# W's units in one load, a new order of the first tiles, `down`'s weights spread, the last four tiles plain: an FNet and GEGLU block on one Trainium2 core

## The chip, the core and the metric

The kernel runs on one core of one Trainium2 chip. The time is device microseconds of one execution; the time before is a median of three runs. TensorE (PE in the profile) multiplies, VectorE (DVE), ScalarE (ACT) and GpSimd (POOL) do the rest, and SyncE (SP) issues every DMA from one queue. Each engine works its instructions off in the order of the program.

## The reference

```python
h  = x + Cr @ (ln(x) @ Wr.T) - Ci @ (ln(x) @ Wi.T)      # Wr, Wi: 448 x 448; Cr, Ci: 2048 x 2048
g  = ln(h) @ w_gate;  u = ln(h) @ w_up                   # 448 x 1792 each
h2 = h + (gelu_tanh(g) * u) @ w_down                     # 1792 x 448
```

x is 2048 x 448 in float32. `Wr`, `Wi` are the DFT matrices along the features, `Cr`, `Ci` those along the sequence; ln is a layer norm without weights.

## The kernel before

**Numbers.** Every product is made in fp16 from a high and a low part of each operand, as three matmuls (high by high, high by low, low by high). ScalarE makes high parts (`hi_part`, L100), VectorE low parts (`lo_part`, L104 or L106). In many places a 2 x 2 block product is made with seven products instead of eight (Strassen's way), which needs sums and differences of blocks first.

**Feature DFT (tiles F).** Sixteen tiles of 128 rows of x are loaded, normed, split (`xs`), turned (`xT`, by PE for tiles 0 to 3, by DMA after that) and multiplied with the feature DFT matrix (`wh_hi`, `wh_lo`; `feature_mm`, L404). Per tile that is 14 matmuls of 448 columns with `wh_hi` and 8 with `wh_lo`, into two banks `ab`. `feature_out` splits the result into `b`.

**Sequence DFT (units U).** Eight passes of eight units. A unit loads a block of W (`wr`, 128 x 4 x 256 float32), splits it into `ws`, and multiplies (`seq_mm`, L491): a plain unit has 24 matmuls of 448 columns, a unit of 5, 6, 7 has 42 of 224 and needs the sums `wsum` (`seq_sums`) before its split. `ws` has three buffers, `wr` four. `seq_out` ends a pass: it adds the accumulators to x in `hx`, the last two additions on GpSimd (L525). Then come the statistics of the norm, and for the first four passes norm, sums, splits and DMA transposes for the later stage.

**What sets the order there.** A list `slots` holds F tiles and units, 80 in all. `plan(n, rank, work)` puts work of the other engines ahead of slot n, by rank within a slot; the numbers in the calls of `plan` are the schedule. Between the units, the gate/up weights are made ready, 14 blocks f, each over three slots: `sums` at n, `split(True)` at n + 1, `split(False)` and the store to `w_dram` at n + 2; the raw load of the next at n + 1.

**Gate/up and down.** 56 steps t, four groups q of 512 rows with 14 blocks f each. In a step `GateUp` makes products X, Y, Z of `gw` and `hops` (L848) and combines them on VectorE (`u`, `hh`, `c`, L858), with gelu on ScalarE and two products on GpSimd. In the first 14 steps there is nothing else for PE; `down`'s weights (`wd`) are loaded, summed on GpSimd (`wd_s`), and split by `down_prep(t - 3)`, two calls per block n of seven. From step 14 on `dn_mm` (L791) multiplies by `wd` with `dn_w`, the split of the hidden tiles, seven products for two row tiles.

**The end.** The last 512 rows' four tiles of `down` are left after step 55. Two are done plainly (`last_mm`, L1011: 28 k-blocks and column halves, three matmuls each, 84 of 224 columns). The other two are a pair with seven products (`last_pair_mm`, 147 matmuls), with sums `last_v`, `last_s` and splits `last_a`.

Of the kernel before, what the change touches and what calls it, by code (L numbers as in the profile page):

```python
# [13 lines left out]
P = 128  # L14
# [18 lines left out]
def kernel(  # L33
# [157 lines left out]
    def down_load(n):  # L191
        wd32[n] = fops.tile([P, 4, HD], F32, tag="xn" if n % 2 else "tt", name=f"wd32_{n}")
        nc.sync.dma_start(wd32[n].rearrange("p (k c) d -> p k (c d)", k=2), w_down[n])
# [100 lines left out]
    first = ExitStack()  # L294
    p1 = first.enter_context(tc.tile_pool(name="p1", bufs=1, side="right"))
# [85 lines left out]
    def wh_high(k):  # L381
        hi_part(wh_hi[:, k, :], wh_raw[k // 2][:, k % 2, :], D_SC)
# [12 lines left out]
    def feature_mm(i, parts=range(2), tag="B"):  # L395
        if 0 in parts:
            feat[i] = [ps_dft.tile([P, 512], F32, tag=tag, name=f"ab{i}_{r}") for r in range(2)]
        steps = [[], [(k, wh_lo, k) for k in range(4)]]
        for k in range(4):
            steps[0] += [(k, wh_hi, k)] + ([(4 + k, wh_hi, k)] if k < 3 else [])  # L400
        for part in parts:
            for n, (kx, w, kw) in enumerate(steps[part]):
                for r in range(2):
                    PE.matmul(  # L404
                        feat[i][r][:, :D],
                        xT[i][:, kx, :],
                        w[:, kw, r * D : (r + 1) * D],
                        start=part == 0 and n == 0,
                        stop=part == 1 and n == 3,
                    )  # L410
# [44 lines left out]
    def seq_load(p, u):  # L455
        wr[p, u] = dft.tile([P, 4, 2 * P], F32, tag="wr", bufs=4, name=f"wr{p}_{u}")
        for g in range(2):
            nc.sync.dma_start(wr[p, u][:, 2 - 2 * g : 4 - 2 * g, :], w_seq[p * N_UNIT + u, :, g::2, :])

    def seq_sums(p, u):  # L460
        r = wr[p, u]
        s = wsum[p, u] = dft.tile([P, 4, 2 * P], F32, tag="wsum", bufs=2, name=f"wsum{p}_{u}")
        V.tensor_add(s[:, 0:2], r[:, 0:1].to_broadcast([P, 2, 2 * P]), r[:, 1:3])  # L463
        V.tensor_add(s[:, 2], s[:, 0], r[:, 2])
        V.tensor_add(s[:, 3], s[:, 2], r[:, 3])  # L465

    def seq_split(p, u):
        r = wr.pop((p, u))
        t = ws[p, u] = dft.tile([P, 2, 7, 2 * P], F16, tag="ws", bufs=3, name=f"ws{p}_{u}")
        parts = [(slice(0, 3), r[:, 1:4]), (slice(3, 7), wsum.pop((p, u)))] if is_s(u) else [(slice(0, 4), r)]  # L470
# [8 lines left out]
    PRODUCTS = [(1, 0, 2, 0), (2, 2, 0, 1), (6, 1, 0, 0), (0, 6, 1, 1), (3, 3, 2, 1), (5, 5, 3, 0), (4, 4, 3, 1)]  # L479

    def seq_mm(p, u, first, last):
# [4 lines left out]
        for cc in range(2):  # L486
# [11 lines left out]
            else:  # L498
                for k, a0 in ((0, 2), (1, 0)):
                    for r in range(2):  # L500
                        for m, (lb, lw) in enumerate(TERMS):
                            rhs = b[:, lb, 2 * r : 2 * r + 2].rearrange("p o d -> p (o d)")
                            mm(k, slice(0, D), w[:, lw, a0 + r, cc * P : (cc + 1) * P], rhs, end and r == 1 and m == 2)
# [8 lines left out]
    def seq_out(p):  # L512
# [11 lines left out]
        for g in range(2):  # L524
            G.tensor_add(h[:, g], h[:, g], e[:, 2 * g : 2 * g + 2].rearrange("p o d -> p (o d)"))  # L525
# [77 lines left out]
    for k, (i, i2) in enumerate(tiles_of):  # L603
        n = where["F", i]
        if k >= 2:
            plan(n - 8, 8, lambda u=i // 2: x_load(u))
            plan(n - 5, 7, lambda i=i, j=i2: x_stats(i, j))
            plan(n - 4, 5, lambda i=i, j=i2: x_rstd(i, j), lambda i=i, j=i2: x_bias(i, j))
            for c in (i, i2):
                n = where["F", c]  # L610
                plan(n - 3, 5, lambda i=c: x_norm(i), lambda i=c: x_lo(i))
                plan(n - 2, 2, lambda i=c: x_turn(i))
# [7 lines left out]
    for g, (p, u) in enumerate(units):  # L620
# [3 lines left out]
        plan(n - 2, 3, lambda p=p, u=u: seq_split(p, u))  # L624
        if g < 4:
            plan(g, 9, lambda p=p, u=u: seq_load(p, u))
# [6 lines left out]
    n0 = p1_end + 4  # L633
    order = list(reversed(range(2, NF))) + [0, 1]
    at_f = [n0 + k * (len(slots) - 3 - n0) // NF for k in range(NF)]
    plan(n0 - 3, 9, lambda: gu.update({order[0]: Weights(order[0])}))
    for k, f in enumerate(order):
# [3 lines left out]
        if k + 1 < NF:  # L641
            plan(n + 1, 9, lambda f=order[k + 1]: gu.update({f: Weights(f)}))
        plan(n + 2, 7, lambda f=f: gu[f].split(False), lambda f=f: gu[f].store())
# [16 lines left out]


    x_load(0, (slice(0, 1),))
    wh_load(0)
    x_load(0, (slice(1, 2),))
    for k in range(1, 4):
        wh_load(k)
    x_load(1)
    x_stats(0)
    wh_high(0)
    x_rstd(0)  # L670
    x_norm(0)
    x_stats(1)
    x_lo(0)
    x_turn_pe(0, 0, 4)
    wh_high(1)
    x_turn_pe(0, 4, 7)
# [3 lines left out]
    wh_high(3)  # L680
    wh_low(3, G)
    x_stats(2, 3)
    x_lo(1)
    feature_mm(0, (0,))
    x_turn_pe(1, 0, 4)
    x_turn_pe(1, 4, 7)
    x_rstd(2, 3)
    x_bias(2, 3)
    x_norm(2)
    x_lo(2)  # L690
    feature_mm(1, (0,))
# [36 lines left out]
    down_load(0)  # L728
# [553 lines left out]
```

## Time and profile before

| | |
|---|---|
| median of 3 runs | 746.25 us (745.68 to 746.96) |
| profiled execution | 745.24 us, span 743.4 us, mean granted clock 0.993 |
| PE busy | 716.3 us (96%) |
| DVE busy | 599.0 us (81%) |
| ACT busy | 329.4 us (44%) |
| POOL busy | 292.8 us (39%) |
| DMA | 142.92 MB, mean 192 GB/s; queue 60.9% busy |

A row of instructions names line, engine, operation, output and inputs, shape and count; a bracket gives the idle time before it and what ended it. "x2" is two instructions in one row. A busy PE is not PE at its full pace, since matmuls overlap; lost time shows better in how long a known number of matmuls takes.

### The profile page before, as it was taken

What the parts mean: (1) busy time and instruction counts of PE and PEld (TensorE: products, weight loads), DVE (VectorE), ACT (ScalarE), POOL (GpSimd) and SP (SyncE); (2) the same over time, 40 slices, a digit from 0 to 9 for tenths busy, and PEclk for the clock granted to TensorE, in tenths of its full rate; (3) what the DMA queues carried; (4) which work ended last, traced back from release to release, by engine and by line L of the source; (5) the groups of instructions that cost most, each with busy time, mean ns of one, the idle gap of its engine ahead of it and who ended that gap; (6) DMA issues with size and microseconds to landing.
All of it is one profiled execution on the core that took longest, in us unless ns stands there. A gap on an engine that the chain in (4) does not pass through costs nothing.

```text
span 743.4 us, 14813 instructions
## 1 busy us (share of the span) xinstructions
PE 716.3 (96%) x5779; PEld 559.1 (75%) x5779; DVE 599.0 (81%) x1165; ACT 329.4 (44%) x611; POOL 292.8 (39%) x316
## 2 busy tenths in 40 slices
PE   7999999998989999999999989999999999999987
PEld 4455557765656666677688868999999999999987
DVE  5677777898989899989447789788787877989795
ACT  5566553537363634444134444345444434444421
POOL 3033121010101020101047986577676766768460
PEclk9999999999999999999999999999999999999999
DMA  9154444788979789786167744656639475555311
GB/s 313 55 126 102 99 119 156 229 233 270 249 255 242 261 227 348 237 303 229 50 207 265 256 173 167 186 182 178 188 128 254 170 213 216 203 187 210 129 38 38
DMA packets 97927, 142.92 MB, mean 192 GB/s; under 512 B 42305, under 2 KB 81345, under 8 KB 97857
## 3 DMA queue, kind: packets, MB, share of 16 engines
q1 hardware_dynamic: 97856, 141.97, 60.9%
q8 instruction: 45, 0.74, 0.4%
q14 instruction: 26, 0.20, 0.1%
HBM read 112.46 MB, written 20.19 MB: 178 GB/s over the span
## 4 chain that ended last, share of the span: by engine, by line
PE 63%; DVE 21%; ACT 5%; DMA 4%; issue 3%; POOL 2%; SPq 1%; ACTq 0%; DVEq 0%; POOLq 0%
PE acc L491 18%; PE pY L848 12%; PE acc_d L791 11%; PE pX L848 8%; PE pZ L848 8%; PE ab L404 6%; DVE ws L106 5%; DVE gu_w L106 2%; DVE xs L104 1%; DVE wsum L463 1%; DMA x<-in_x_dram 1%; DMA gw<-w_dram 1%; DVE dn_w L104 1%; ACT ws L100 1%; DVE last_v L1032 1%
## 5 line engine op out<-in xcount | busy, mean ns | idle before, releaser
L491 PE MATMUL acc<-b,ws 128*128 128x448 f16 (+1 forms) x1968 | 282.7, 305 | 7.6 <-DVE ws L106 6.8
L491 PEld LDWEIGHTS <-ws 128*128 128x128 f16 x1968 | 188.8, 98 | 100.8 <-DVE ws L106 13.1
L848 PEld LDWEIGHTS <-gw 128*128 128x128 f16 x2067 | 202.3, 98 | 30.2 <-issue 6.5
L848 PE MATMUL pY<-hops,gw 128*128 128x256 f16 x901 | 123.2, 273 | 5.5 <-DVE u L858 5.2
L525 POOL TENSOR_TENSOR hx<-hx,e 128x448 f32<-128x448 f32 x16 | 25.2, 1594 | 253.3 <-DVE e L522 158.6
L791 PE MATMUL acc_d<-wd,dn_w 128*128 128x224 f16 x882 | 105.4, 259 | 0.0
L106 DVE SCALAR_TENSOR_TENSOR ws<-wr,ws 128x1024 f16<-128x1024 f32 (+1 forms) x64 | 76.7, 1199 | 15.0 <-ACT ws L100 14.8
L791 PEld LDWEIGHTS <-dn_w 128*128 128x128 f16 x882 | 85.2, 98 | 3.0
L100 ACT ACTIVATE ws<-wr 128x1024 f16<-128x1024 f32 (+1 forms) x64 | 61.6, 969 | 50.1 <-PE acc L491 25.2
L848 PE MATMUL pX<-hops,gw 128*128 128x256 f16 x583 | 81.3, 273 | 1.7 <-DMA gw<-w_dram 1.7
L848 PE MATMUL pZ<-hops,gw 128*128 128x256 f16 x583 | 79.7, 274 | 0.0
L858 DVE SCALAR_TENSOR_TENSOR u<-pY,u 128x256 f32<-128x256 f32 x112 | 47.0, 420 | 36.6 <-PE pY L848 18.2
L886 ACT ACTIVATE u<-pX 128x256 f32<-128x256 f32 x56 | 21.4, 382 | 90.4 <-PE pX L848 84.9
L404 PEld LDWEIGHTS <-xT 128*128 128x128 f16 x352 | 34.4, 99 | 34.3 <-issue 2.3
L915 POOL TENSOR_TENSOR hh<-hh,g 128x256 f32<-128x256 f32 x42 | 35.9, 855 | 57.8 <-DVE hh L858 57.8
L104 DVE TENSOR_TENSOR dn_w<-dn_s,dn_w 128x640 f16<-128x640 f32 x42 | 52.7, 1254 | 1.6 <-ACT dn_w L100 1.4
L899 ACT ACTIVATE g<-pX 128x256 f32<-128x256 f32 x56 | 21.3, 380 | 70.0 <-PE pX L848 66.5
L404 PE MATMUL ab<-wh_hi,xT 128*128 128x448 f16 x224 | 47.0, 360 | 1.1 <-DVE b L106 0.7
L100 ACT ACTIVATE ws<-wsum 128x1024 f16<-128x1024 f32 x24 | 25.3, 1054 | 50.9 <-DVE wsum L465 50.9
L941 POOL TENSOR_TENSOR dn_s<-hh 128x256 f32<-128x256 f32 x42 | 43.5, 1036 | 0.0
L924 POOL TENSOR_TENSOR hh<-hh,c 128x256 f32<-128x256 f32 x42 | 36.8, 877 | 16.3 <-ACT c L922 16.3
L942 POOL TENSOR_TENSOR dn_s<-hh 128x256 f32<-128x256 f32 x42 | 43.1, 1026 | 0.0
(134 smaller groups left out, 956.8 us busy)
## 6 DMA issues: line engine op xcount, KB each, us to landing
gw<-w_dram SPq DMA_DIRECT2D x53, 896.0 KB, 5.0
wr<-in_w_seq_dram SPq DMA_DIRECT2D x128, 256.0 KB, 4.9
w_dram<-gu_w SPq DMA_DIRECT2D x14, 896.0 KB, 4.8
gu_raw<-in_w_gu_dram SPq DMA_DIRECT2D x28, 384.0 KB, 4.7
wd<-in_w_down_dram SPq DMA_DIRECT2D x14, 448.0 KB, 4.9
hx<-in_x_dram SPq DMA_DIRECT2D x8, 448.0 KB, 5.8
h_dram<-hx SPq DMA_DIRECT2D x8, 448.0 KB, 5.2
hr<-h_dram SPq DMA_DIRECT2D x8, 448.0 KB, 5.4
```

What stands on the lines that cost most here:

```text
L100: A.activation(dst, src, AF.Copy, scale=scale)
L104: V.tensor_sub(dst, src, hi)
L106: V.scalar_tensor_tensor(dst, src, scale, hi, op0=ALU.mult, op1=ALU.subtract)
L404: PE.matmul(feat[i][r][:, :D], xT[i][:, kx, :], w[:, kw, r * D : (r + 1) * D], start=part == 0 and n == 0, stop=part == 1 and n == 3,)
L491: PE.matmul(banks[k][:, cols], lhs, rhs, start=k not in begun, stop=stop, skip_group_check=True)
L791: PE.matmul(acc[k // 2][:, k % 2 * HD : (k % 2 + 1) * HD], a_of(la, a), b_of(lb, b), start=first and m == 0 and k % 2 == 0, stop=last and ...
L848: PE.matmul(ps, w[:, wl, wa + ws, :], ops[:, m + ms, :], start=first and n == 0, stop=last and n == len(terms) - 1, skip_group_check=True,)
L858: V.scalar_tensor_tensor(dst, ps, SC, other, op0=ALU.mult, op1=ALU.add)
L915: G.tensor_mul(c21, c21, self.g1)
L924: G.tensor_mul(c22, c22, self.c12)
L941: G.tensor_add(s[:, 0:2], t[:, 0:2], t[:, 2:4])
L942: G.tensor_sub(s[:, 2:4], t[:, 1:4:2], t[:, 0:4:2])
```

## The change

- Each unit of W comes in one DMA of 512 KB in the order in which it lies in memory, instead of two; the quarters are named anew in `seq_sums`, `seq_split`, `PRODUCTS` and `seq_mm`, and a unit with sums is split in three pieces instead of two.
- `feature_mm` of one tile is cut into eleven steps in place of two parts; at the start PE's order mixes the steps of tiles 0, 1, 2 with the turns of tiles 1, 2, 3. GpSimd makes the fourth block of `wh_hi`, the first two tiles of x are loaded ahead of all of `wh`, and x loads, statistics, norms and turns of later tiles are planned two slots earlier.
- One gate/up block's weights are made ready among the feature tiles (slot 14); the other thirteen follow from slot 24 on, the last at slot 71 instead of 73. The raw load moves from n + 1 to n + 2 and the store from n + 2 to n + 3.
- `seq_out`'s last two additions run on VectorE.
- `down`'s first load and sums stand in the sequence passes; `down_prep` runs two steps earlier.
- The last four tiles of `down` are all made by `last_mm`; the pair's code is gone.

```diff
-    def feature_mm(i, parts=range(2), tag="B"):
+    def feature_mm(i, part=range(11), tag="B"):
...
+        steps = [(k, wh_hi, n) for k, n in ((0, 0), (1, 1), (4, 0), (5, 1), (2, 2), (6, 2), (3, 3))]
+        steps += [(k, wh_lo, k) for k in range(4)]
...
     def seq_load(p, u):
         wr[p, u] = dft.tile([P, 4, 2 * P], F32, tag="wr", bufs=4, name=f"wr{p}_{u}")
-        for g in range(2):
-            nc.sync.dma_start(wr[p, u][:, 2 - 2 * g : 4 - 2 * g, :], w_seq[p * N_UNIT + u, :, g::2, :])
+        nc.sync.dma_start(wr[p, u], w_seq[p * N_UNIT + u])
...
-        parts = [(slice(0, 3), r[:, 1:4]), (slice(3, 7), wsum.pop((p, u)))] if is_s(u) else [(slice(0, 4), r)]
+        parts = [(slice(0, 1), r[:, 0:1]), (slice(1, 3), r[:, 2:4]), (slice(3, 7), wsum.pop((p, u)))] if is_s(u) else [(slice(0, 4), r)]
...
         for g in range(2):
-            G.tensor_add(h[:, g], h[:, g], e[:, 2 * g : 2 * g + 2].rearrange("p o d -> p (o d)"))
+            V.tensor_add(h[:, g], h[:, g], e[:, 2 * g : 2 * g + 2].rearrange("p o d -> p (o d)"))
...
-    n0 = p1_end + 4
+    pairs = [where["F", 2 * u] for u in ORDER if is_s(u)]
+    early_f = [s + 4 for s in pairs[1:2]]
+    n0 = p1_end + 3
...
         plan(n + 1, 7, lambda f=f: gu[f].split(True))
         if k + 1 < NF:
-            plan(n + 1, 9, lambda f=order[k + 1]: gu.update({f: Weights(f)}))
-        plan(n + 2, 7, lambda f=f: gu[f].split(False), lambda f=f: gu[f].store())
+            plan(n + 2, 9, lambda f=order[k + 1]: gu.update({f: Weights(f)}))
+        plan(n + 2, 7, lambda f=f: gu[f].split(False))
+        plan(n + 3, 10, lambda f=f: gu[f].store())
...
+    plan(len(slots) - 14, 9, lambda: down_load(0))
+    plan(len(slots) - 8, 9, lambda: down_sums(0))
...
-    wh_high(3)
+    x_lo(1)
     wh_low(3, G)
-    x_stats(2, 3)
-    x_lo(1)
-    feature_mm(0, (0,))
+    feature_mm(0, range(6))
+    x_stats(2)
     x_turn_pe(1, 0, 4)
     x_turn_pe(1, 4, 7)
...
-            if t == 2:
-                down_sums(0)
-            if t > 2:
-                down_prep(t - 3)
+            if t > 0:
+                down_prep(t - 1)
...
-        if t - 3 <= 2 * NC:
-            down_prep(t - 3)
+        if t == 2 * NC:
+            down_prep(t - 1)
...
+    for n, (j, g) in enumerate(((0, 0), (0, 1), (1, 0))):
+        last_mm(j, g, banks[n : n + 1])
         do(N_GU + 1 + n, 3)
...
-        last_pair_mm(n)
...
+        last_out(j, g, banks[n], 0, 2)
+    last_mm(1, 1, banks[3:])
```

The end of pass 2 on VectorE before: `acc2` are the pass's banks, `hx2` its rows, `e2` helper sums, `ws3` and `wsum3` the next pass's W.

```order
L520 SCALAR_TENSOR_TENSOR hx2_1870<-acc2_1_1753,hx2_1870 128x448
L521 SCALAR_TENSOR_TENSOR e2_2139<-acc2_3_1755,e2_2139 128x224
L522 SCALAR_TENSOR_TENSOR e2_2139<-acc2_2_1754,e2_2139 128x224
L523 SCALAR_TENSOR_TENSOR e2_2139<-acc2_2_1754,e2_2139 128x224
L106 SCALAR_TENSOR_TENSOR ws3_1_2149<-wr3_1_1976,ws3_1_2149 128x1024
L463 TENSOR_TENSOR wsum3_6_2152<-wr3_6_2011 128x512
L464 TENSOR_TENSOR wsum3_6_2152<-wsum3_6_2152,wr3_6_2011 128x256
```

The same place on VectorE now (lines are three further down):

```order
L523 SCALAR_TENSOR_TENSOR hx2_1885<-acc2_1_1774,hx2_1885 128x448
L524 SCALAR_TENSOR_TENSOR e2_2154<-acc2_3_1776,e2_2154 128x224
L525 SCALAR_TENSOR_TENSOR e2_2154<-acc2_2_1775,e2_2154 128x224
L526 SCALAR_TENSOR_TENSOR e2_2154<-acc2_2_1775,e2_2154 128x224
L528 TENSOR_TENSOR hx2_1885<-hx2_1885,e2_2154 128x448 x2
L106 SCALAR_TENSOR_TENSOR ws3_1_2164<-wr3_1_1998,ws3_1_2164 128x1024
L466 TENSOR_TENSOR wsum3_6_2167<-wr3_6_2031 128x512
```

The two additions (L528) now stand on VectorE ahead of the split of the next unit; before, they were GpSimd's and ran beside that split.

VectorE at steps 14 and 15 of gate/up before: `wd` is written by a low part of `down`'s weights, `dn_w` by one of the hidden tiles, `u3` and `u2` are what PE waits for.

```order
L106 SCALAR_TENSOR_TENSOR wd_4085<-wd_s_5_4927,wd_4085 128x1120
L104 TENSOR_TENSOR dn_w1_5017<-hh0_4106,dn_w1_5017 128x256
L104 TENSOR_TENSOR dn_w1_5017<-dn_s1_4944,dn_w1_5017 128x640
L858 SCALAR_TENSOR_TENSOR u3_14_5047<-pY_14_4965,u1_14_4978 128x256
L858 SCALAR_TENSOR_TENSOR hh1_4999<-pZ_14_5003,u3_14_5047 128x256
L943 TENSOR_TENSOR dn_s2_5050<-hh0_4106 128x128
L217 SCALAR_TENSOR_TENSOR nb_h2_0_5065<-mv_h2_0_3019,r_h2_0_3028 128x2
L858 SCALAR_TENSOR_TENSOR hh1_4999<-pY_14_4965,u1_14_4978 128x256
L858 SCALAR_TENSOR_TENSOR c12_14_5081<-pZ_14_5003,u2_14_4980 128x256
L858 SCALAR_TENSOR_TENSOR u2_15_5102<-pY_15_5087,u1_15_5100 128x256
L106 SCALAR_TENSOR_TENSOR wd_4085<-wd32_6_4925,wd_4085 128x448
L104 TENSOR_TENSOR dn_w2_5120<-hh0_4106,dn_w2_5120 128x256
```

The same place on VectorE now:

```order
L106 SCALAR_TENSOR_TENSOR wd_4080<-wd_s_6_4926,wd_4080 128x1120
L104 TENSOR_TENSOR dn_w1_5012<-hh0_4101,dn_w1_5012 128x256
L104 TENSOR_TENSOR dn_w1_5012<-dn_s1_4943,dn_w1_5012 128x640
L882 SCALAR_TENSOR_TENSOR u3_14_5042<-pY_14_4964,u1_14_4977 128x256
L882 SCALAR_TENSOR_TENSOR hh1_4998<-pZ_14_5002,u3_14_5042 128x256
L967 TENSOR_TENSOR dn_s2_5045<-hh0_4101 128x128
L217 SCALAR_TENSOR_TENSOR nb_h2_0_5060<-mv_h2_0_3023,r_h2_0_3032 128x2
L882 SCALAR_TENSOR_TENSOR hh1_4998<-pY_14_4964,u1_14_4977 128x256
L882 SCALAR_TENSOR_TENSOR c12_14_5076<-pZ_14_5002,u2_14_4979 128x256
L882 SCALAR_TENSOR_TENSOR u2_15_5097<-pY_15_5082,u1_15_5095 128x256
L104 TENSOR_TENSOR dn_w2_5112<-hh0_4101,dn_w2_5112 128x256
```

At step 14 a `wd` split still stands ahead of `dn_w1` (block 6's in place of block 5's); at step 15 the one ahead of `dn_w2` is gone, and so is step 16's.

161 lines of the change are left out of this document (68 added, 93 removed).

## The prediction

> **What bounds the kernel now.** I read the busy times stage by stage first, then who TensorE (PE) waited for, then the order of time at those places. The stages: the first three feature tiles, the rest of the feature DFT, the later sequence passes, the first gate/up block, the other blocks, the end. Columns of the first six rows: the stretch, its length, busy time of PE, its weight loads, VectorE (DVE), ScalarE (ACT) and GpSimd (POOL), the granted clock, DMA.
>
> ```profile
> 0.00:27.20 27.20, 21.46 (x144) 12.93 (x145) 13.25 (x40) 15.33 (x27) 5.90 (x10) 0.94 0.67 230
> 27.20:104.50 77.30, 76.45 (x445) 43.08 (x443) 58.65 (x124) 45.75 (x73) 20.16 (x18) 1.00 0.42 101
> 156.80:289.00 132.20, 124.80 (x872) 82.57 (x871) 120.59 (x228) 61.31 (x93) 13.34 (x8) 1.00 0.88 255
> 371.60:465.00 93.40, 86.68 (x781) 76.53 (x779) 68.00 (x131) 39.68 (x85) 65.89 (x69) 0.98 0.61 213
> 465.00:704.80 239.80, 239.31 (x2289) 222.12 (x2288) 198.82 (x400) 102.23 (x242) 163.39 (x188) 1.00 0.59 189
> 704.80:743.40 38.60, 32.72 (x318) 30.74 (x315) 29.17 (x57) 7.49 (x12) 14.53 (x17) 0.96 0.10 37
> ...
> 104.50:138.60 34.10, 34.10 (x244) 23.47 (x243) 1.00 0.52 158
> ...
> PE acc L491 <- DVE ws L106: 6.8, 16, 1.1
> PE pY L848 <- DVE u L858: 5.2, 5, 2.3
> PE acc_d L791 <- DVE last_a L104: 3.0, 3, 2.1
> PE pX L848 <- DMA gw<-w_dram: 1.7, 2, 1.3
> ```
>
> PE bounds the kernel, and what it loses is lost at five places. From 465 to 704.8 us it loses nothing, and the change does not touch that. In the sequence passes an undisturbed stretch ran 244 matmuls in 34.10 us; the 872 of 156.8 to 289 us need 872 x 34.10 / 244 = 121.9 us at that pace and took 132.2. So 10.3 us are lost there, more than the wait rows name, and there VectorE is busy 120.6 of 132.2 us, the rest being its own waits: VectorE is the bound of that stretch. In the first gate/up block PE waits for VectorE's `u`, at the end for `last_a`.
>
> **The end (last four tiles plain): -3.4 us.**
>
> ```profile
> 704.74 8.05 PEld L1011 LDWEIGHTS <-h_last 128*128 128x128 f16 x84
> 718.08 2.49 PE L791 MATMUL acc_d<-wd,last_a 128*128 128x224 f16 x13 [2.14 <-DVE last_a L104]
> ...
> 710.00:720.00 10.00, 7.86 (x73) 7.07 (x72) 9.90 (x16) 2.21 (x3) 8.27 (x10) 0.91 0.06 20
> ...
> 732.43 4.03 PE last_X L1011 x42
> 736.45 4.04 PE last_Y L1011 x42
> ```
>
> One plain tile is 84 matmuls of 224 columns and takes 8.05 us, paced by its weight loads. Before, the end held two such tiles and, for the other two, seven products of 21 matmuls, 147 in all; now it holds four plain tiles, 336 matmuls for 315. The 21 more cost 2.0 us. But the pair now needs no sums and splits (VectorE 9.90 of 10 us in the row, with waits of PE up to 2.14 us and a clock of 0.91 behind them). Four tiles from 704.8 us take 4 x 8.05 = 32.2 us, to 737.0; before, the last tile ended at 736.45 + 4.04 = 740.5. What follows it (a half tile's sum, a store) is the same. Nothing is late next: the last hidden tile's low part is needed at the end of the first plain tile, as before.
>
> **Passes' sums to VectorE, W in one load: -3.0 us.** Each pass ends with two additions that move from GpSimd to VectorE (instructions L525).
>
> ```profile
> 158.00 3.20 POOL L525 TENSOR_TENSOR hx<-hx,e 128x448 f32<-128x448 f32 x2 [31.32 <-DVE e L522]
> ...
> 158.08 2.13 DVE L106 SCALAR_TENSOR_TENSOR ws<-wr,ws 128x1024 f16<-128x1024 f32 x1
> 160.13 1.62 DVE L463 TENSOR_TENSOR wsum<-wr 128x512 f32<-128x512 f32 x1
> 162.59 0.55 DVE L543 TENSOR_TENSOR gu_s<-gu_raw 128x384 f32<-128x384 f32 x1
> 186.87 1.22 DVE L106 SCALAR_TENSOR_TENSOR ws<-wr,ws 128x1024 f16<-128x1024 f32 x1
> 188.00 0.69 DVE L463 TENSOR_TENSOR wsum<-wr 128x512 f32<-128x512 f32 x1
> 189.52 1.28 DVE L106 SCALAR_TENSOR_TENSOR gu_w<-gu_s,gu_w 128x512 f16<-128x512 f32 x2
> ```
>
> While GpSimd adds, the same VectorE instructions take 2.13 and 1.62 us that take 1.22 and 0.69 elsewhere: 0.91 + 0.93 = 1.84 us. The additions on VectorE have 448 columns, between 384 (0.55) and 512 (0.69): 0.62 each, less the overlap of neighbours, 1.15 for two. VectorE gains 0.7 us at a pass end; the eight POOL instructions of the stretch are four such ends: 2.8 us. Against it, a unit with sums is now split in three pieces instead of two: two pieces of 512 take 1.28, one of 1024 takes 1.22, so about 0.07 more for each of some 11 units: 0.8 us. ScalarE's extra piece lies in its 61 busy of 132 us. Of the gate/up weights' preparation one unit moves into the feature stage and the others shift by a slot, which takes about a quarter of a unit (L543 to its last split, some 4 us by these rows) out of the stretch: 1.0 us. Together 2.8 - 0.8 + 1.0 = 3.0. Ends: all 10.3 us if VectorE's waits for ScalarE go too; a loss of 4 x 1.15 + 0.8 = 5.4 if the stretching has another cause and stays. I stay with the row that shows it.
>
> The Trainium skill ("SBUF — State Buffer", on the shared port pair) says that GpSimd and a VectorE instruction with two SBUF inputs take the pair exclusively and the loser blocks for the whole instruction. By that, each end would cost 3.2 us and the gain were 4 x (3.2 - 1.15) = 8.2 instead of 2.8, the sum 5.4 lower; the row shows 1.84 of 3.2, so the trace agrees on the contention, not on the full block.
>
> One DMA per unit of W instead of two halves SyncE's issues; no PE wait there names a load, and of VectorE's four kinds of wait in the stretch the second row below is the only one for a DMA, so I cost the merged load at nothing: the four buffers that run ahead cover it, and without them a landing is some 5 us. The weights' raw load moves one slot later, the store behind it another; the next sums stand two slots on, two units of the 8 in a pass of 34 us, some 8 us, and the load lands in 4.7 (last column of the first row).
>
> ```profile
> gu_raw<-in_w_gu_dram SPq DMA_DIRECT2D x28, 384.0 KB, 4.7
> ...
> DVE gu_s L543 <- DMA gu_raw<-in_w_gu_dram: 0.5, 1, 0.5
> ```
>
> **First tiles' order: -2.3 us.**
>
> ```profile
> 9.97 1.79 ACT L100 ACTIVATE wh_hi<-wh_raw 128x896 f16<-128x896 f32 x2
> 11.12 0.63 DVE L314 BATCH_NORM_STATS2 st_x<-x 128x6 f32<-128x448 f32 x1 [1.97 <-DMA x<-in_x_dram]
> 11.85 2.44 POOL L390 TENSOR_SCALAR wh_raw<-wh_raw 64x896 f32<-64x896 f32 x1 [9.60 <-ACT wh_hi L100]
> 24.48 0.39 PE L369 MATMUL xT_ps<-ident,xs 128*128 128x128 f16 x4
> 27.23 2.81 PE L404 MATMUL ab<-wh_hi,xT 128*128 128x448 f16 x14
> ...
> 58.65 8.29 PE ab L404 x43
> ```
>
> Tile 3 began at 27.23 us. Now PE puts tile 1's and 2's transposes between matmuls, and the fourth block of the hidden DFT's high part is made by GpSimd: it stands for 2.44 us (the nearest row has the same width on half the partitions). Its data landed by 10.8, since ScalarE worked on it without a wait; more likely about 10. So PE passes that matmul pair at 12.5 to 13.3. By then 12 of the 66 matmuls of tiles 0 to 2 are done; 54 remain at 8.29 / 43 = 0.193 us, 10.4 us, and two turns of seven transposes, about 0.6 each by the row and its sibling. 12.8 + 10.4 + 1.2 = 24.4, and 0.5 for small waits: 24.9, so -2.3. Ends: 0 if VectorE's chain of statistics for tiles 2 and 3 (they wait for x at 11.12) sets the pace, -3.5. The rest of the feature stage loses 0.85 us of PE now; x, norms and turns come two slots earlier, one gate/up unit (4 us of VectorE, 58.65 busy of 77.30) is added, and I leave it as it is, within 1 us either way.
>
> **Gate/up's first block: -2.3 us.**
>
> ```profile
> 373.10 0.38 DVE L523 SCALAR_TENSOR_TENSOR e<-acc,e 128x224 f32<-128x224 f32 x1
> 374.14 0.82 PE L848 MATMUL pY<-hops,gu_w 128*128 128x256 f16 x6
> 376.00 1.04 SPq L193 DMA_DIRECT2D wd<-in_w_down_dram  x2
> 384.78 0.83 PE L848 MATMUL pX<-hops,gw 128*128 128x256 f16 x6 [1.30 <-DMA gw<-w_dram]
> 441.89 1.23 PE L848 MATMUL pY<-hops,gw 128*128 128x256 f16 x5 [2.29 <-DVE u L858]
> 446.92 1.25 DVE L106 SCALAR_TENSOR_TENSOR wd<-wd,wd 128x448 f16<-128x448 f32 x1
> 450.69 0.71 PE L848 MATMUL pY<-hops,gw 128*128 128x256 f16 x5 [0.78 <-DVE u L858]
> 453.99 1.61 DVE L106 SCALAR_TENSOR_TENSOR wd<-wd_s,wd 128x1120 f16<-128x1120 f32 x1
> 458.12 0.71 PE L848 MATMUL pY<-hops,gw 128*128 128x256 f16 x5 [1.00 <-DVE u L858]
> ```
>
> `down`'s splits run two steps earlier. At steps 15 and 16 the `wd` splits of 1.25 and 1.61 us vanish from VectorE's queue ahead of `u`, and with them the waits of 0.78 and 1.00: -1.8. The wait of 2.29 us at step 14 stays: a `wd` split and `dn_w` stand ahead of `u` as before. One of the two `down` loads at 376.0 moves ahead, so the weights that PE waited 1.30 us for get the queue sooner: -1.3. But the last pass's two additions now stand on VectorE between L523 and the first `u`: 1.15 us, and PE's second pY of 374.14 needs it at once: +0.8. GpSimd's first `wd_s` sums go into the sequence passes, where it is idle.
>
> **Sum.** -3.4 - 3.0 - 2.3 - 2.3 = -11.0 us on the profiled execution of 745.24 us (span 743.4, 1.84 around it), which is 734.2; the median of the runs lies 1.01 higher: 735.2 us.
>
> **Rivals.** (a) The passes gain nothing, because pieces and additions give back what GpSimd's absence brings: 738.2. For it: the terms are small against 132 us; against it: the stretched rows. (b) VectorE gets ahead and its waits for ScalarE go with it, most of the 10.3 us: 728 to 731. For it: a queue that is full; against it: the norm's chain through ScalarE is unchanged. The clock belongs here: the skill's "TensorE: Matmul & The Clock Gate" (part 1, the clock gate) has windows of 3.4 us that run freely and half rate after one idle window; the trace fell to half after waits of only 2.14 and 2.29 us. As the phase is free, the fall behind step 14's wait may go, 1.7 us less, 733.5; I count it to the range. (c) The start gains nothing or the feature stage pays it back: 737.5 to 739. (d) Slower: in the stretch that VectorE bounds, every sum of gate/up weights waits for its raw load, now issued a slot later behind SyncE's queue. Seven units stand there; from 1.6 us of wait each it eats all 11.0, and at 2 us the time is 749. One such wait of 0.5 us exists now; against it stands the distance of some 8 us to a landing of 4.7.
>
> **How the numbers follow.** The forecast with its parts near their values: 0.62; (a) 0.14; (b) 0.10; (c) 0.08; (d) 0.06, of which 0.04 end slower and 0.02 within the bound. Less than 0.2% of the time (1.5 us) is about what a measurement of this kernel cannot tell from no change. Faster by more 0.94, within 0.02, slower 0.04. The range from 731 to 740 leaves out (d), and the further half of (b).
>
> **What would show it.** End: 84 weight loads in 8.05 us four times over, clock 1.00, no wait for `last_a`. Passes: no L525 on POOL, `ws` at 1.22 behind `seq_out`, fewer than 10.3 us lost. Start: tile 3 near 25 us. First block: no waits at steps 15 and 16, 2.3 us at 14, and a new one below 1 us at the first pY. Wrong would make it: new waits of VectorE for `gu_raw`, or of PE in the feature stage.

## The result and the profile after

The changed kernel takes 738.66 us (736.13 to 740.09, four runs) where the kernel before, in four runs, takes 746.40: a ratio of 0.9891 with a 95% interval of 0.9875 to 0.9908. The forecast was 735.2 us in a range of 731 to 740. The profiled execution is the shortest of the four, 736.13 us with a span of 734.3. For half of the four the mean granted clock is 0.998 and for half 0.993, which fits the half rate described at the end of this document: it comes in some runs and not in others.

The stages of the profile after, cut at the same events as in the table below (columns as in the prediction's first fence: stretch, length, busy time of PE, its weight loads, VectorE, ScalarE, GpSimd, granted clock, DMA):

```profile
0.00:28.56 28.56, 20.90 (x144) 13.34 (x145) 18.34 (x57) 13.98 (x27) 8.79 (x11) 0.94 0.58 210
28.56:111.64 83.08, 81.13 (x467) 45.33 (x466) 59.15 (x120) 47.83 (x80) 20.48 (x18) 1.00 0.50 126
111.64:370.07 258.43, 254.14 (x1789) 172.02 (x1788) 227.50 (x447) 117.17 (x190) 4.28 (x3) 1.00 0.73 233
370.07:434.10 64.03, 62.02 (x565) 55.02 (x564) 46.83 (x93) 27.66 (x60) 44.13 (x46) 1.00 0.69 238
434.10:698.92 264.82, 262.02 (x2504) 243.05 (x2502) 219.47 (x441) 114.12 (x267) 181.21 (x208) 1.00 0.58 187
698.92:734.30 35.38, 32.36 (x338) 32.11 (x336) 6.28 (x12) 1.20 (x3) 6.85 (x10) 1.00 0.11 40
```

| stage | before | after | difference | forecast |
|---|---|---|---|---|
| until tile 3's first matmul | 27.23 | 28.56 | +1.33 | -2.3 |
| from there to slot 22 (feature stage) | 81.65 | 83.08 | +1.43 | 0, within 1 |
| slots 22 to 79 (passes) | 262.75 | 258.43 | -4.32 | -3.0 |
| gate/up steps 0 to 13 | 64.88 | 64.03 | -0.85 | -0.5 |
| from the first `dn_mm` (step 14) to the end's first matmul | 268.33 | 264.82 | -3.51 | -1.8 |
| the end | 38.56 | 35.38 | -3.18 | -3.4 |
| span | 743.4 | 734.3 | -9.1 | -11.0 |

Whom PE waited for, after (waited for, total, times, longest); the first row is new in this size, and `last_a` and the DMA of `gw` are gone:

```profile
PE xT_ps L370 <- ACT xT L371: 5.8, 4, 2.3
PE pY L872 <- DVE u L882: 4.5, 4, 2.3
PE acc L494 <- DVE ws L106: 4.4, 10, 0.7
PE ab L408 <- DVE b L106: 1.7, 4, 0.9
```

The start, timeline of after. Of VectorE's two splits of `wh` in the second row the first takes 2.02 us, beside a GpSimd instruction (first row), and the other its usual 1.08. VectorE reaches the statistics of tiles 10 and 11 late, and ScalarE's square root `sd_x` for them waits 2.24 us. Behind it in ScalarE's queue stand `b` of tile 0 and the copy `xT` of tile 3's turn, for which PE waits 2.34 us:

```profile
16.43 1.99 POOL L396 TENSOR_TENSOR wh_lo<-wh_raw,wh_hi 64x896 f16<-64x896 f32 x1
17.35 3.02 DVE L106 SCALAR_TENSOR_TENSOR wh_lo<-wh_raw,wh_hi 128x896 f16<-128x896 f32 x2
...
24.43 0.29 ACT L121 ACTIVATE sd_x<-mv_x,eps_t 128x2 f32<-128x2 f32 x1 [2.24 <-DVE mv_x L316]
24.63 0.96 ACT L100 ACTIVATE b<-ab 128x448 f16<-128x448 f32 x2
25.48 0.60 ACT L371 ACTIVATE xT<-xT_ps 128x512 f16<-128x512 f16 x1
26.13 0.33 PE L370 MATMUL xT_ps<-ident,xs 128*128 128x128 f16 x3 [2.34 <-ACT xT L371]
```

The feature stage, at the border of slots 10 and 11, repeats it: ScalarE stood 3.76 us before a square root, its part of `feature_out` came behind, and PE waited 0.89 us for the bank.

```profile
63.19 0.29 ACT L121 ACTIVATE sd_x<-mv_x,eps_t 128x2 f32<-128x2 f32 x1 [3.76 <-DVE mv_x L316]
63.40 0.96 ACT L100 ACTIVATE b<-ab 128x448 f16<-128x448 f32 x2
64.63 0.35 PE L408 MATMUL ab<-wh_hi,xT 128*128 128x448 f16 x1 [0.89 <-DVE b L106]
```

The end of pass 2 on VectorE, after: the two additions, then the split and the sum at their usual 1.22 and 0.69 us, not 2.13 and 1.62.

```profile
160.61 1.15 DVE L528 TENSOR_TENSOR hx<-hx,e 128x448 f32<-128x448 f32 x2
161.68 1.22 DVE L106 SCALAR_TENSOR_TENSOR ws<-wr,ws 128x1024 f16<-128x1024 f32 x1
162.81 0.69 DVE L466 TENSOR_TENSOR wsum<-wr 128x512 f32<-128x512 f32 x1
```

The last wait of gate/up's first block, at step 14, and the weight loads of all four last tiles (a group: count, busy time, mean ns): 32.2 us, four times 8.05.

```profile
439.48 0.70 PE L872 MATMUL pY<-hops,gw 128*128 128x256 f16 x5 [2.29 <-DVE u L882]
```

```profile
L1035 PEld LDWEIGHTS <-h_last 128*128 128x128 f16 x336 | 32.2, 98 | 0.0
```

### The profile page after: what moved, and what is told of

Its sections match the earlier page's. It is cut to its first block, busy times and chain, and to the rows that moved or that the text cites. A ratio compares the mean times of both kernels' runs of the same rounds, so it can differ in the third digit from the quotient of the medians.

```text
span 734.3 us, 14677 instructions
## 1 busy us (share of the span) xinstructions
PE 712.6 (97%) x5800; PEld 560.9 (76%) x5800; DVE 577.6 (79%) x1166; ACT 322.0 (44%) x624; POOL 265.7 (36%) x294
## 4 chain that ended last, share of the span: by engine, by line
PE 65%; DVE 19%; ACT 7%; DMA 4%; issue 4%; POOL 2%; SPq 1%; ACTq 0%; DVEq 0%; POOLq 0%
PE acc L494 19%; PE pY L872 13%; PE acc_d L815 11%; PE pX L872 8%; PE pZ L872 8%; DVE ws L106 4%; DVE xs L104 2%; ACT ws L100 2%; DMA w_dram<-gu_w 2%; DVE gu_w L106 2%; ACT b L100 2%; DMA x<-in_x_dram 1%; PE last_Z L1035 1%; PE last_X L1035 1%; PE last_tr L1035 1%
## 5 line engine op out<-in xcount | busy, mean ns | idle before, releaser
L198 POOL TENSOR_TENSOR wd_s<-wd 128x448 f32<-128x448 f32 x7 | 8.0, 1144 | 217.0 <-DMA wd<-in_w_down_dram 217.0
L106 DVE SCALAR_TENSOR_TENSOR ws<-wr,ws 128x1024 f16<-128x1024 f32 (+2 forms) x88 | 74.6, 871 | 14.8 <-ACT ws L100 14.2
L100 ACT ACTIVATE ws<-wr 128x1024 f16<-128x1024 f32 (+2 forms) x88 | 63.7, 756 | 49.3 <-issue 30.3
```

The source lines that it names most:

```text
L100: A.activation(dst, src, AF.Copy, scale=scale)
L106: V.scalar_tensor_tensor(dst, src, scale, hi, op0=ALU.mult, op1=ALU.subtract)
```

## The experiments

The first nine kernels alter the changed kernel in one thing or two; the last three build on one another. A ratio is against runs of the kernel before on the same chip. "Tile 3" and "slot 22" are their first matmuls in the one profiled execution of each kernel; "steps 14 on" runs to the end's first matmul. Since there is one profile for each kernel, the columns show how far they repeat: the passes lie between 258.37 and 258.58 us in the six kernels that change nothing there, but tile 3 begins between 28.13 and 29.47 in the six that have the changed start, and between 26.41 and 28.75 in the three that share start_no_gpsimd's. A single difference of 1 or 2 us at tile 3 shows little.

| kernel | median, us (lowest to highest) | ratio to before, 95% | tile 3 | slot 22 | passes | steps 14 on |
|---|---|---|---|---|---|---|
| before | 746.40 (745.68 to 746.96) | | 27.23 | 108.88 | 262.75 | 268.33 |
| after | 738.66 (736.13 to 740.09) | 0.9875 to 0.9908 | 28.56 | 111.64 | 258.43 | 264.82 |
| start_undone | 735.55 (734.39 to 736.18) | 0.9834 to 0.9871 | 28.89 | 110.54 | 258.58 | 265.06 |
| stats_late | 742.09 (739.93 to 743.36) | 0.9926 to 0.9961 | 26.16 | 113.79 | 258.53 | 266.26 |
| x_in_slots | 737.82 (733.97 to 740.45) | 0.9848 to 0.9901 | 27.73 | 110.95 | 258.42 | 264.82 |
| x_in_slots_wh3_act | 738.96 (737.95 to 739.70) | 0.9881 to 0.9907 | 29.31 | 112.53 | 258.42 | 266.30 |
| sums_gpsimd | 742.39 (740.51 to 744.24) | 0.9929 to 0.9964 | 28.13 | 111.33 | 262.67 | 266.57 |
| gu_undone | 737.98 (737.30 to 738.43) | 0.9874 to 0.9905 | 28.60 | 111.26 | 259.92 | 264.80 |
| w_two | 746.28 (742.91 to 748.67) | 0.9970 to 0.9999 | 29.47 | 114.28 | 263.39 | 264.90 |
| w_two_gu_undone | 738.20 (737.63 to 738.47) | 0.9869 to 0.9907 | 28.43 | 111.08 | 259.94 | 264.82 |
| down_undone | 740.88 (739.35 to 741.57) | 0.9908 to 0.9934 | 29.24 | 110.96 | 258.81 | 268.31 |
| start_no_gpsimd | 735.67 (734.79 to 736.98) | 0.9834 to 0.9875 | 27.72 | 109.36 | 258.37 | 266.30 |
| units_moved | 728.93 (727.88 to 731.32) | 0.9744 to 0.9791 | 26.41 | 108.05 | 251.99 | 266.30 |
| down_earlier | 727.95 (726.10 to 730.06) | 0.9730 to 0.9767 | 28.75 | 110.40 | 251.99 | 263.44 |

### The start and the feature stage

**start_undone.** The hand-written order, the plan of x and W's first loads as before:

```diff
-    feature_mm(0, range(6))
-    x_stats(2)
+    x_stats(2, 3)
+    x_lo(1)
+    feature_mm(0, range(7))
...
-                plan(n - 7, 7, lambda i=i, j=i2: x_stats(i, j))
+            plan(n - 5, 7, lambda i=i, j=i2: x_stats(i, j))
```

> The changed kernel with the order of the first tiles, the plan of x and the first loads of W as before; all else of the change stays. Theory A (the new order of the start costs the 1.3 us at tile 3 and the 1.4 us of the feature stage, since the norms of later tiles stand ahead of feature_out on ScalarE and VectorE): tile 3 begins near 27.2 us instead of 28.5, the waits of slots 10, 11 fall to those of before, the span is 2.7 us shorter (near 731.6 where the clock dips no more often). Rival B (the gate/up unit that moved among the feature tiles, or W in one load, costs the 1.4 us): tile 3 at 27.2, but the feature stage from there to slot 22 still 83 us long, the span 1.3 shorter.

The interval lies wholly below that of the changed kernel: by the medians the new start costs 3.1 us. In the profile the feature stage is back at 81.65 us, with the early gate/up unit and the single load of W still there. So theory A holds for the feature stage and rival B falls. Tile 3, however, begins at 28.89, not at 27.2, in the old order, so the profile does not show where the rest of the 3.1 us lies. At this start the last of VectorE's small steps for tile 2's and 3's `r_x` took 1.73 us beside an instruction of GpSimd; the group's row (least, median and most of nine, in ns) has 0.16 us for its median:

```profile
13.96 1.91 POOL L396 TENSOR_TENSOR wh_lo<-wh_raw,wh_hi 64x896 f16<-64x896 f32 x1
...
14.16 1.73 DVE L132 SCALAR_TENSOR_TENSOR r_x<-r_x 128x2 f32<-128x2 f32 x1
```

```profile
L132 DVE SCALAR_TENSOR_TENSOR r_x<-r_x x9: 158/160/1728, 5.2 to 85.3; 128x2 f32<-128x2 f32 x7, 128x1 f32<-128x1 f32 x2
```

**stats_late.** The copies of tile 3's turn ahead of tile 0's `feature_out` and of the statistics of tiles 10 and 11:

```diff
-    x_stats(a, b)
-    x_rstd(a, b)
-    x_bias(a, b)
...
-    feature_out(0)
     feature_mm(1, range(7, 9))
     x_turn_pe(3, 0, 4)
     x_turn_pe(3, 4, 7)
+    feature_out(0)
+    x_stats(a, b)
+    x_rstd(a, b)
+    x_bias(a, b)
```

> The changed kernel; at the start the statistics of tiles 10 and 11 and tile 0's feature_out stand behind tile 3's turn, no longer ahead of it. Theory A1 (ScalarE's copies of tile 3's turn wait in its queue behind a square root that VectorE feeds late): PE's wait of 2.34 us there falls to about 0.7, tile 3 begins at 26.9 us instead of 28.5, the span is 1.6 us shorter. Rival A2 (VectorE's work of the start, drawn out by GpSimd's instructions beside it, sets the pace wherever the statistics stand): tile 3 moves by less than 0.5 us, and the wait turns up at feature_out's bank.

Tile 3 did begin 2.4 us earlier, at 26.16, and 2.0 earlier than in any kernel that has the changed start: A1 is right on what delayed it. But the run is 3.4 us slower. The statistics now come late for the norm of tile 10 on ScalarE, the norms stand ahead of the first split of W, and PE waits 3.04 us for that split at slot 4. From 33.8 us on the clock is at half for 3.4 us, and the feature stage is 4.6 us longer in all:

```profile
29.03 0.76 ACT L336 ACTIVATE x<-x,nb_x,r_x 128x448 f32<-128x448 f32 x1 [1.02 <-DVE nb_x L328]
...
32.43 1.04 ACT L100 ACTIVATE ws<-wr 128x1024 f16<-128x1024 f32 x1
...
33.52 0.70 PE L494 MATMUL acc<-b,ws 128*128 128x448 f16 x2 [3.04 <-ACT ws L100]
```

**x_in_slots.** The mixed start kept; x from the third pair on planned as before, `wh_load(0)` second:

```diff
-    a, b = tiles_of[2]
-    x_stats(a, b)
-    x_rstd(a, b)
-    x_bias(a, b)
...
-                plan(n - 4, 2, lambda i=c: x_turn(i))
+                plan(n - 2, 2, lambda i=c: x_turn(i))
```

> The changed kernel with its mixed order of tiles 0 to 3 at the start, but with the x tiles from the third pair on in the plan of before (load, statistics, norm and turn 8, 5, 3 and 2 slots ahead), wh's first block loaded ahead of the second tile of x as before, and tile 3's turn ahead of feature_out(0). Theory A (two things cost: the norms planned two slots earlier, and at the start what stands ahead of the copies on ScalarE): tile 3 begins at 26.3 us or up to 0.7 earlier, the feature stage from there is 81.7 us long as before, slot 22 begins near 108 instead of 111.6, the run is 3.5 us faster than the changed kernel. Rival: the waits in the feature stage come with W in one load or the early gate/up unit; then slots 10, 11 still lose 1.4 and 0.3 us and slot 22 begins near 109.5.

The losses of slots 10 and 11 shrink as theory A says (1.39 and 0.34 to 0.34 and 0), but tile 3 begins at 27.73 and tile 10's turn is late at slot 5 (last row), so that the feature stage still takes 83.22 us, against 83.08. By the times it is not told apart from the changed kernel. Two `xs` splits of VectorE that take 0.69 us elsewhere took 2.37, again beside L396:

```profile
15.08 1.87 POOL L396 TENSOR_TENSOR wh_lo<-wh_raw,wh_hi 64x896 f16<-64x896 f32 x1
15.14 2.37 DVE L104 TENSOR_TENSOR xs<-x,xs 128x64 f16<-128x64 f32 x2
...
38.23 2.06 PE L408 MATMUL ab<-wh_hi,xT 128*128 128x448 f16 x10 [1.63 <-DMA xT<-xs]
```

**x_in_slots_wh3_act.** In addition `wh_high(3)` on ScalarE:

```diff
-    wh_high(3, G)
...
+    wh_high(3)
```

> As x_in_slots, and ScalarE makes the fourth block of wh_hi, as before, not GpSimd. If GpSimd's longer work at the start (2.78 us for that block, then the low part) draws out VectorE's splits of wh (1.51 us each against 1.03) and its small steps, VectorE reaches the statistics of tile 3 about 1 us earlier and tile 3 begins up to 1 us earlier than in x_in_slots. If PE does not wait for VectorE there any more: no difference at tile 3 (within 0.3 us).

Tile 3 begins 1.6 us later, with a stretch of half clock of 3.4 us ahead of it that the other profile does not have. Half of that stretch, 1.7 us, is the whole difference. GpSimd's L396 only hits another instruction of VectorE, a split of `wh` that takes 1.08 us elsewhere:

```profile
13.95 1.90 POOL L396 TENSOR_TENSOR wh_lo<-wh_raw,wh_hi 64x896 f16<-64x896 f32 x1
14.03 2.76 DVE L106 SCALAR_TENSOR_TENSOR wh_lo<-wh_raw,wh_hi 128x896 f16<-128x896 f32 x1
```

### The passes

**sums_gpsimd.**

```diff
-            V.tensor_add(h[:, g], h[:, g], e[:, 2 * g : 2 * g + 2].rearrange("p o d -> p (o d)"))
+            G.tensor_add(h[:, g], h[:, g], e[:, 2 * g : 2 * g + 2].rearrange("p o d -> p (o d)"))
```

> The changed kernel with seq_out's last two additions on GpSimd again. By the prediction's row (GpSimd draws out VectorE's neighbours by 1.84 us, the two additions on VectorE cost 1.15) the passes from slot 22 on get 2.8 us longer over four pass ends that PE feels; by a full block of VectorE 8.2 us longer; if the additions are worth nothing, 0, and then the 4.3 us that the passes gained come from the other parts.

4.24 us longer, between the two prices. The row is back as it was: 1.84 us more on VectorE's two instructions at each pass end.

```profile
161.05 3.20 POOL L528 TENSOR_TENSOR hx<-hx,e 128x448 f32<-128x448 f32 x2 [30.70 <-DVE e L525]
161.13 2.13 DVE L106 SCALAR_TENSOR_TENSOR ws<-wr,ws 128x1024 f16<-128x1024 f32 x1
163.19 1.61 DVE L466 TENSOR_TENSOR wsum<-wr 128x512 f32<-128x512 f32 x1
```

**gu_undone.**

```diff
-    early_f = [s + 4 for s in pairs[1:2]]
-    n0 = p1_end + 3
+    n0 = p1_end + 4
...
-            plan(n + 2, 9, lambda f=order[k + 1]: gu.update({f: Weights(f)}))
-        plan(n + 2, 7, lambda f=f: gu[f].split(False))
-        plan(n + 3, 10, lambda f=f: gu[f].store())
+            plan(n + 1, 9, lambda f=order[k + 1]: gu.update({f: Weights(f)}))
+        plan(n + 2, 7, lambda f=f: gu[f].split(False), lambda f=f: gu[f].store())
```

> The changed kernel with the gate/up weights' preparation placed as before (no unit among the feature tiles, fourteen from slot 25 on, load and store a slot earlier). By the prediction the passes lose 1.0 us of their gain. Rival: where a unit stands against a pass end decides, not the sum of VectorE's work; then the losses move to other slots and the passes change by 2 us or more in either direction. The wait of 0.42 us at slot 21 should go only if the early unit causes it.

The passes are 1.49 us longer, the feature stage 0.42 shorter, for the wait at slot 21 is gone. That is near the forecast's 1.0; the losses did move among the slots, but not by 2 us in sum. In the medians the two cannot be told apart.

**w_two.**

```diff
-        nc.sync.dma_start(wr[p, u], w_seq[p * N_UNIT + u])
+        for g in range(2):
+            nc.sync.dma_start(wr[p, u][:, 2 - 2 * g : 4 - 2 * g, :], w_seq[p * N_UNIT + u, :, g::2, :])
```

> The changed kernel with W in two loads per unit and in the old order of its quarters, two pieces to a split instead of three. By the prediction the third piece costs 0.8 us in the passes and the loads nothing: the passes get 0.8 us shorter, the feature stage stays. Rival: 64 more DMA issues on SyncE's queue make other transfers late (gu_raw, x), and VectorE or PE waits for them: 1 us or more longer.

The surprise of the study: 746.28 us, nearly all of the change's gain gone. In the profile the passes are 5.0 us longer, the feature stage 1.7, the first steps of gate/up 1.4 and the start 0.9. In the passes VectorE waits for gate/up's raw weights (columns as in PE's waits), here at 236.55 us, and PE behind it for `ws`:

```profile
DVE gu_s L547 <- DMA gu_raw<-in_w_gu_dram: 7.2, 5, 2.1
```

```profile
236.55 0.56 DVE L547 TENSOR_TENSOR gu_s<-gu_raw 128x384 f32<-128x384 f32 x1 [2.07 <-DMA gu_raw<-in_w_gu_dram]
...
243.02 1.31 PE L495 MATMUL acc<-b,ws 128*128 128x448 f16 x6 [1.41 <-DVE ws L106]
```

In the changed kernel the same wait is 0.4 us in all. This is rival (d) of the prediction, in its place and with its mechanism; W's single load keeps it off.

The 1.7 us of the feature stage are another wait, all of them in slots 19 to 21. There ScalarE writes a feature tile (`b`, as `b32` in the code) into a buffer that it shares (tag `w`) with the early gate/up block's weights, and it may start only when these are stored to `w_dram`. With two loads of W that store comes later. PE then waits 0.85 us for the tile and 0.69 for the next split; in the changed kernel only 0.24 at that split are left of it.

```profile
103.88 0.98 ACT L100 ACTIVATE b<-ab 128x448 f32<-128x448 f32 x2 [9.37 <-DMA w_dram<-gu_w]
104.47 3.05 PE L408 MATMUL ab<-wh_hi,xT 128*128 128x448 f16 x14 [0.85 <-ACT b L100]
```

**w_two_gu_undone.** Both of the last two edits.

> The changed kernel with both W in two loads (as in w_two, whose passes were 5.0 us longer) and the gate/up preparation placed as before (as in gu_undone, 1.5 us longer). Theory I (the one load is worth nothing by itself, it only covers the gate/up raw load that now stands a slot later behind SyncE's loads of W): with the raw load early again VectorE's waits for gu_raw fall from 7.2 us to under 1, and the passes take 259 to 260 us. Rival II (two loads per unit cost by themselves, as SyncE or the DMA engines are slower with them): 5.0 + 1.5 us over the changed kernel's 258.4, 264 to 265.

Theory I: 259.94 us, as gu_undone's 259.92. With the gate/up plan of before, two loads and two pieces take as long as one load and three pieces; load and piece were not changed apart, so a small cost of the one could hide a small gain of the other. One wait for `gu_raw` is left, longer than expected (gu_undone has one of 1.0):

```profile
DVE gu_s L547 <- DMA gu_raw<-in_w_gu_dram: 1.6, 1, 1.6
```

Whether SyncE's issues or the transfers themselves delay the raw load behind two loads of W was not separated: in w_two a unit's issue takes 1.21 us where one load takes 0.33, and the raw load's median time to landing is 6.0 us, against 5.3 in the changed kernel.

### Down's weights

**down_undone.**

```diff
-            if t > 0:
-                down_prep(t - 1)
+            if t == 2:
+                down_sums(0)
+            if t > 2:
+                down_prep(t - 3)
```

> The changed kernel with down's first load behind the passes, its first sums at step 2 and down_prep(t - 3) again. By the prediction the waits of 0.78 and 1.00 us at steps 15 and 16 come back, and the wait for gate/up's weights behind down's second load (1.30 us): together 3.1 us longer, up to 1.7 more or less where the clock's dip behind step 14 differs. Rival: steps 15 and 16 wait for something else, or the two loads collide no more: under 1 us.

From step 14 on it takes 3.5 us more, though the clock does not dip there in either profile; the two waits are 1.56 and 1.00 us, and one of 0.64 for `hh` comes with them. PE never waits for `gw`, although `down`'s load stands behind the passes again: that part of the expectation is wrong.

```profile
442.04 0.81 PE L871 MATMUL pY<-hops,gw 128*128 128x256 f16 x6 [0.64 <-DVE hh L881]
448.00 0.71 PE L871 MATMUL pY<-hops,gw 128*128 128x256 f16 x5 [1.56 <-DVE u L881]
455.43 0.71 PE L871 MATMUL pY<-hops,gw 128*128 128x256 f16 x5 [1.00 <-DVE u L881]
```

### Towards a faster kernel

**start_no_gpsimd.** start_undone without GpSimd at the start:

```diff
-    wh_low(3, G)
...
-    for k in range(3):
+    for k in range(4):
         wh_low(k)
```

> As start_undone, and VectorE makes the low part of wh's fourth block, so that GpSimd does nothing between 3 and 30 us. Theory (in start_undone GpSimd's TENSOR_TENSOR of 1.91 us held a VectorE step of 0.16 us for 1.73 us, and this chain set tile 3's start): no step of r_x longer than 0.2 us, tile 3 at 27.3 us (1.4 earlier) unless the clock dips there. Rival: the fourth low part on VectorE (about 1.03 us) makes it late for xs of tile 3, and tile 3 begins no earlier than 28.3.

No `r_x` step is drawn out, and GpSimd has nothing to do at the start after its first memory fill. Tile 3 begins at 27.72 us with 3.4 us of half clock around 11 us, at 26.41 in the next kernel, which has the same start and no dip there, and at 28.75 in the last, with a dip from 15.3 us on. The times show no difference from start_undone (735.67 against 735.55): the stall of that profile is not shown to cost on average.

**units_moved.** In addition the gate/up blocks' slots by hand:

```diff
-    at_f = early_f + [n0 + k * (len(slots) - 5 - n0) // late_f for k in range(late_f)]
+    at_f = [14, 20, 24, 30, 37, 45, 53, 56, 59, 62, 65, 68, 71, 74]
...
-            plan(n + 2, 9, lambda f=order[k + 1]: gu.update({f: Weights(f)}))
+            plan(n + (1 if at_f[k + 1] - n < 4 else 2), 9, lambda f=order[k + 1]: gu.update({f: Weights(f)}))
```

> As start_no_gpsimd, with the gate/up blocks' slots written out: 14, 20, 24, 30, 37, 45, 53, then every third to 74, so that fewer stand between slots 31 and 55, and none beside the sums of the feed-forward's norm; where the next block follows after three slots its raw load stands a slot earlier. If VectorE's sum of work between slots 31 and 60 is what holds PE: the 6.4 us lost at slots 38 to 60 fall to about 3, the run is 3 us faster than start_no_gpsimd. Rival: the units every third slot hold PE in turn (a unit is 4.2 us of VectorE, a slot 4.3, W's splits 2.2 a slot), and nothing is won.

All of the 6.4 us went, not half: from slot 22 to the first gate/up step PE is busy in every moment, 251.98 of 251.98 us, with VectorE at 89% of the stretch. VectorE's work there fell only from 225.96 to 224.52 us, and its waits for `gu_raw` are 0.8 us against 0.7: the gain comes mainly from where the work stands, not from its sum or from the loads. The run is 6.7 us faster than start_no_gpsimd, 728.93 us, and beats both kernels.

```profile
108.06:360.04 251.98, 251.98 (x1789) 172.95 (x1788) 224.52 (x443) 117.86 (x190) 3.71 (x3) 1.00 0.73 238
```

**down_earlier.** In addition:

```diff
-            if t > 0:
-                down_prep(t - 1)
+            down_prep(t)
```

> As units_moved, with every step of down_prep one gate/up step earlier (t instead of t - 1), so that none stands at step 14. If the last low part of down's weights, ahead of dn_w on VectorE, makes the wait of 2.29 us at step 14: VectorE's queue there gets 1.5 us shorter, the wait falls to 0.8 or less, and the half clock behind it may go too (1.7 us): 1.5 to 3.2 us faster than units_moved. Rival: dn_w waits for GpSimd's sums of the hidden tile (dn_s) through ScalarE; then the wait falls by less than 0.5 us. Against both: the first block's new low part at step 0 can make PE wait at its first u, by up to 1 us.

Step 14's wait fell from 2.29 to 1.09 us, and the wait 12 us ahead of it rose from 1.31 to 2.76: it moved. At 727.95 us it is not told apart from units_moved.

```profile
421.67 1.23 PE L855 MATMUL pY<-hops,gw 128*128 128x256 f16 x5 [2.76 <-DVE u L865]
433.40 0.70 PE L855 MATMUL pY<-hops,gw 128*128 128x256 f16 x5 [1.09 <-DVE u L865]
```

## Why the prediction was right or wrong

The time lies in the range and the sign is right, but 3.5 us above the forecast. Of these, 1.9 are the sum of the stages in the table above (the start and the feature stage 5.1 us worse, all else 3.2 better), and 1.5 are that the profiled execution now stands 2.5 us below the median, not 1.0.

- **First tiles' order, -2.3: wrong, and rival (c) came about.** The step that failed is "12.8 + 10.4 + 1.2 = 24.4, and 0.5 for small waits". It counted PE's work and took the other engines as ready: GpSimd's block of `wh_hi` took 2.78 us, not 2.44, and was done at 13.82, and PE's waits for ScalarE's copies `xT` alone are 5.8 us. The end it named, 0 if VectorE's chain of statistics sets the pace, was the nearer one: the chain stood ahead of PE's copies in ScalarE's queue (stats_late moved tile 3 by 2.4 us). No kernel with the changed start has tile 3 before 28.13. That the new order is worse than the old one at tile 3, by 1.33, is not shown, since start_undone has 28.89. "I leave it as it is, within 1 us" for the feature stage failed for the same reason: work planned two slots earlier is work put ahead of `feature_out` (start_undone took the 1.43 us back).
- **Passes, -3.0: right in mechanism, 1.3 short.** Taken apart by w_two_gu_undone and gu_undone, which differ from before in the sums but not in the gate/up plan: the sums gained 2.8 us (262.75 to 259.9), just as forecast, though `down`'s first load and sums, which are new in these passes too, are in this number; the third piece and W's single load together cost 0, not 0.8; the gate/up plan gained 1.5, not 1.0. In the changed kernel's own plan the sums are worth 4.2.
- **W in one load, "at nothing": right alone, wrong in company.** The cover named was the four buffers and the distance of some 8 us. The runs showed that the distance holds only with the single load; without it rival (d) costs the passes 5.0 us, and the late store of the early gate/up block, of which the prediction says nothing, 1.7 us of the feature stage.
- **Gate/up's first block, -2.3.** The waits at steps 15 and 16 went (-1.8), 2.29 us at step 14 stayed, and a new wait of 0.63 us came at the second pY (+0.8 forecast). The half clock behind step 14 went too, 1.7 us, which stood in the range only. The -1.3 for `gw` has no support: down_undone has no such wait, while start_undone, x_in_slots, gu_undone and others, with the load ahead, have 0.7 to 1.7 us of it. It comes and goes.
- **The end, -3.4: right.** 3.18 us, and 35.4 us in each of the twelve altered kernels. It was not tried alone.

## What to carry to other kernels

Before work is moved earlier, write down for every engine in its path what it will now stand ahead of, and when its own input comes: an instruction that waits at the head of a queue costs what is behind it, and stats_late shows that mending one place can push the wait to the next. A part that is worth nothing by itself may still be the cover of another: taking W's single load back cost 7.6 us with the new gate/up plan and nothing with the old one, so undo parts in pairs before calling one idle. Where an engine's work holds PE over a stretch, spreading it (units_moved, 6.4 us) can be worth more than any one part of a change like this.

## What the runs showed of the hardware

**Some instructions of GpSimd and VectorE shut each other out.** Three starts show one GpSimd instruction of 1.87 to 1.91 us, and each time the VectorE instruction that began 0.06 to 0.2 us behind it took 1.6 to 1.7 us longer (0.16 to 1.73, 0.69 to 2.37, 1.08 to 2.76): it stood until GpSimd was done. So the rule of the Trainium skill ("SBUF — State Buffer", on the shared port pair: the loser blocks for the whole instruction) agrees with these rows, and the prediction read its row wrongly. The 3.20 us of GpSimd's two additions hold GpSimd's own waiting for VectorE; by themselves they take 1.13 us each, the least of these 16 in the kernel before (ns: least, median, most), and VectorE's 1.84 us of delay at a pass end stand against twice 1.13, not against 3.20. The start of the changed kernel is a fourth case: its split of 2.02 us began 0.92 us behind L396 and took 0.94 us longer than the other.

```profile
L525 POOL TENSOR_TENSOR hx<-hx,e x16: 1127/1577/2197, 123.8 to 374.4; 128x448 f32<-128x448 f32 x16
```

It is not every pair. VectorE's combinations `u`, which read one input from a PSUM bank, took their usual 0.42 us beside GpSimd in the kernel before (first two rows below); the fourteen profiles have some 900 that began while a two-input instruction of GpSimd ran, and none was more than 0.02 us longer than the shortest. And in the changed kernel a split of `wh` took its usual 1.08 us inside GpSimd's one-input L395 of 2.45 us (last two rows).

```profile
420.33 0.73 POOL L941 TENSOR_TENSOR dn_s<-hh 128x256 f32<-128x256 f32 x1
420.58 0.42 DVE L858 SCALAR_TENSOR_TENSOR u<-pY,u 128x256 f32<-128x256 f32 x1 [0.30 <-PE pY L848]
...
13.90 2.45 POOL L395 TENSOR_SCALAR wh_raw<-wh_raw 64x896 f32<-64x896 f32 x1
15.00 1.08 DVE L106 SCALAR_TENSOR_TENSOR wh_lo<-wh_raw,wh_hi 128x896 f16<-128x896 f32 x1
```

**Whether a wait brings the half clock depends on how it lies to a grid of 3.41 us.** The wait of 2.3 us at step 14 is followed by 3.4 us at half clock in the profiles of before, stats_late, sums_gpsimd, x_in_slots_wh3_act, start_no_gpsimd and units_moved, and not in those of after, start_undone, x_in_slots, gu_undone, w_two, w_two_gu_undone and down_undone. Where only this differs, "steps 14 on" is 264.8 to 265.1 us without it and 266.3 to 266.6 with it. Inside one profile all changes of the clock lie whole multiples of 3.413 us apart (in the kernel before at 4.86, 8.27, 11.68, 441.76, 445.18, 718.24 and 721.65 us). Counted on this grid, the nine waits that the half clock followed (six at step 14; 2.14 us at the end of before, 3.04 in stats_late, 2.76 in down_earlier) had at least 2.14 us of the wait in one window. In the seven that it did not follow, the wait was cut by a window's border, and no window held more than 1.78 us of it. The limit lies somewhere between, as far as these sixteen waits show. The windows around step 14, of before and then of after (stretch, length, PE, weight loads, VectorE, ScalarE, GpSimd, clock, DMA):

```profile
438.35:441.76 3.41, 1.25 (x13) 1.07 (x12) 2.89 (x4) 1.40 (x3) 3.41 (x3) 1.00 0.38 158
441.76:445.17 3.41, 3.28 (x16) 2.31 (x16) 3.21 (x6) 0.74 (x2) 3.41 (x5) 0.50 0.00 0
...
435.12:438.53 3.41, 2.07 (x21) 1.81 (x19) 2.89 (x4) 1.63 (x4) 3.41 (x4) 1.00 0.58 235
438.53:441.95 3.42, 2.47 (x23) 2.24 (x23) 3.21 (x7) 0.96 (x3) 2.92 (x4) 1.00 0.09 17
```

The borders fall differently in each profile. A kernel with waits of this size would then scatter by steps of about 1.7 us, and the four times of the changed kernel with their two clocks fit this, which is why terms below 2 us were read from the stages here and not from the times.
